# A new written-out sequence of steps, and 255 engine choices, in an mLSTM and gated-FFN kernel

## The chip, the cores and the metric

The kernel runs on one core of one Trainium2 chip. The metric is the time of one execution on the device in microseconds, taken as the median of three runs; one more execution was profiled.

## The reference

Two stages follow each other. The first is an mLSTM cell over 4 batches, 8 heads, 768 steps and head size 40; the second is a gated feed-forward layer over the 3072 tokens that the first one gives.

```python
m_new = np.maximum(f_gate[:, :, t] + m, i_gate[:, :, t])
f_stab = np.exp(f_gate[:, :, t] + m - m_new)
i_stab = np.exp(i_gate[:, :, t] - m_new)
C = f_stab * C + i_stab * einsum('bhd,bhe->bhde', vt, kt)
n = f_stab * n + i_stab * kt
h_tilde = einsum('bhde,bhe->bhd', C, qt)
y[:, :, t] = sigmoid(o_gate) * h_tilde / np.maximum(np.abs(n . qt), 1.0)
...
gate = 1.0 / (1.0 + np.exp(-(x @ w_gate)))     # x: 3072 x 320, w_gate, w_val: 320 x 1536
val = x @ w_val
return gate * val @ w_out                      # w_out: 1536 x 320
```

The weights arrive as 64-bit floats, seen by the kernel as pairs of 32-bit words.

## The kernel before, in words

**Tiling.** The 768 steps are cut into 6 chunks of 128 (c = 0 to 5), so there are 24 units (c, b) of one chunk and one batch; unit u is 4c + b. For a unit the attention takes these steps: q and k are turned (`a`, copied out by `ah`), scores are multiplied (`b`) and masked decays multiplied in (`bm`, VectorE, L1110 or L782), they are applied to v (`c`, tile `av`), the sum is normed (`cv`, `cg`, `cr`; `cr` at L842 writes tile `x`), the last 64 columns of `x` are doubled (`cx`, L850), the result is turned (`d`, tile `xt`) and split in a high part `xh` (`dx`) and a low part `xl` (`dy`, L880). Each chunk also updates a state `cst` (`z`, `zm`, `zd`, `za`) from k weighted by the decay (`bk`, L757). Every product of the feed-forward layer is done with high and low parts: w = wh + wl, x = xh + xl, three products of four.

**The feed-forward tiles.** There are 103 tiles, called 0 to 102. Tile n takes 128 of the 1536 columns for two or four batches of a chunk. Its up-projection `t` is 16 matmuls at L951, 256 or 512 columns wide, eight into bank `pg0` and eight into `pg1`. Then follow `ta` (tanh of pg0, ScalarE, L964), `tg` (the gate times pg1, VectorE, L967), `th` (high part, ScalarE or VectorE), `tl` (low part, VectorE or GpSimd, L978) and the down-projection `p`, three matmuls of 320 columns for each batch at L989. `pg0` and `pg1` exist once. So the next tile's matmuls into pg0 need `ta` of this one, and those into pg1 need its `tg`. Chunk 0 has tiles 0 to 3 (batches 0 and 1), 4 to 7 (batches 2 and 3), and 8 to 15 (all four).

**The weights** are decoded piece by piece: step `a` on ScalarE, three steps `b` on VectorE (L540, L544, L548), the high part `d` and the low part `e` (L589, L593, L595). Pieces are called g, v, r for the first three and 3 to 29 for the rest. One piece holds the columns of two tiles.

**What sets the order.** Nothing is scheduled by a program: the string `ORDER` names every step in turn, and each engine gets its instructions in that order. Each engine runs its own list in order and waits where it needs another's result. The table `eng` in `PARAM` says for a step on which engine it stands: p is GpSimd, v VectorE, a ScalarE. A `/` in `ORDER` swaps which of two PSUM banks the next small tile takes. DMAs are issued by SyncE in the order of the list, those of q for the first unit by ScalarE.

Of the kernel before, what the change touches and what calls it, by code (L numbers as in the profile page):

```python
# [28 lines left out]
        'cm1': 'a', 'cp00': 'a', 'cp02': 'v', 'qb2': 'v', 'ro': 'v', 'xd0': 'v', 'bk0': 'p', 'cx0': 'v', 'bk1': 'p',  # L29
        'cr1': 'v', 'cx1': 'v', 'wve': 'p', 'w3e': 'p', 'w4e': 'p', 'w5e': 'v', 'w6e': 'v', 'w7e': 'p', 'w8e': 'p',  # L30
        'w10e': 'v', 'w11e': 'v', 'w13e': 'v', 'w16e': 'v', 'w17e': 'p', 'w18e': 'p', 'w19e': 'p', 'w20e': 'v',
        'w21e': 'p', 'w23e': 'p', 'w25e': 'p', 'aq2.0': 'v', 'ah2.1': 'a', 'aq2.1': 'v', 'ah2.2': 'a', 'bk2': 'p',
        'cr2': 'p', 'cx2': 'p', 'zm2.1': 'v', 'aq3.0': 'v', 'ah3.1': 'a', 'aq3.1': 'v', 'cr3': 'p', 'zm3.1': 'a',
        'aq4.0': 'v', 'ah4.1': 'v', 'aq4.1': 'v', 'aq4.2': 'p', 'bd4': 'v', 'cr4': 'v', 'dx4': 'v', 'aq5.0': 'v',
        'ah5.1': 'a', 'bk5': 'v', 'zd5.1': 'p', 'tl1': 'p', 'tl2': 'p', 'tl10': 'p', 'arg': 'a', 'w24e': 'p',
        'w27d': 'a', 'za4.0': 'v', 'zm5.0': 'v', 'za5.0': 'v', 'zm5.1': 'a', 'ah6.0': 'a', 'ah6.2': 'v', 'aq6.2': 'v',
        'bd6': 'p', 'za6.0': 'p', 'zd6.1': 'v', 'ah7.0': 'a', 'ah7.1': 'a', 'ah7.2': 'a', 'bk7': 'v', 'cx7': 'p',
        'zm7.0': 'a', 'zd7.0': 'p', 'za7.0': 'p', 'aq8.0': 'a', 'aq8.2': 'v', 'bd8': 'v', 'cr8': 'p', 'cx8': 'v',
        'zm8.0': 'v', 'zd8.0': 'p', 'zm8.1': 'v', 'zd8.1': 'p', 'za8.1': 'v', 'aq9.0': 'a', 'e9a': 'p', 'dx9': 'a',
        'zm9.0': 'a', 'zd9.0': 'p', 'za9.0': 'v', 'zd9.1': 'v', 'aq10.0': 'a', 'cr10': 'p', 'zm10.1': 'v',  # L40
# [1167 lines left out]
```

## Time and profile before

| what | us |
|---|---|
| median of 3 runs (lowest to highest) | 514.95 (514.45 to 516.51) |
| the profiled execution: its time, its span | 513.81, 511.8 |
| TensorE busy with matmuls | 503.7 |
| TensorE loading weights (beside the matmuls) | 458.4 |
| VectorE, ScalarE, GpSimd busy | 318.6, 200.8, 164.3 |

The span goes from the first to the last instruction; the time has 2.0 us around it. Busy time of one engine lies beside that of the others. A matmul's end is modelled, so a busy TensorE is not one at its peak.

### The profile page before, as it was taken

The page shows a single profiled execution, that of the slowest core. Times are in us where ns is not written, and L with a number is a line of the kernel's source. Part 1 is how long each engine was busy: PE and PEld are TensorE (multiplying, and loading weights), DVE is VectorE, ACT ScalarE, POOL GpSimd, SP SyncE. Part 2 cuts the span into 40 slices and gives each one's busy share as a digit, 9 for nine tenths or more (in the row PEclk, how much of TensorE's full clock was granted, in tenths as well). Part 3 has the DMA queues.
Part 4 walks back from the last instruction along what each step waited for, and adds up shares of the span by engine and source line. Part 5 has one row for each costly group of instructions (what it writes and reads, how often), then busy time and mean ns, then how long its engine had stood idle before and what let it go on. Part 6 is the DMA issues. An engine that isn't in the chain of part 4 may idle for free.

```text
span 511.8 us, 12224 instructions
## 1 busy us (share of the span) xinstructions
PE 503.7 (98%) x4671; PEld 458.4 (90%) x4671; DVE 318.6 (62%) x767; ACT 200.8 (39%) x530; POOL 164.3 (32%) x226
## 2 busy tenths in 40 slices
PE   7899999999999999999999999999999999999997
PEld 6788988889999999988888888888888888999997
DVE  8899998997647667565867366676444434442222
ACT  5987765674423332353332322213432411222321
POOL 3563334557730231342225322432241311101111
PEclk9999999999999999999999999999999999999999
DMA  9997768789889695977887788769759730000000
GB/s 196 240 274 192 200 192 221 168 141 189 191 179 172 136 216 119 199 150 156 186 161 180 146 189 195 160 127 190 165 118 198 155 87 5 27 28 1 28 0 27
DMA packets 227578, 75.55 MB, mean 148 GB/s; under 512 B 207040, under 2 KB 215424, under 8 KB 227520
## 3 DMA queue, kind: packets, MB, share of 16 engines
q1 hardware_dynamic: 226432, 74.51, 66.4%
q8 instruction: 37, 0.61, 0.5%
q10 hardware_dynamic: 1088, 0.26, 0.3%
q14 instruction: 21, 0.17, 0.1%
HBM read 57.61 MB, written 17.14 MB: 146 GB/s over the span
## 4 chain that ended last, share of the span: by engine, by line
PE 94%; DVE 3%; DMA 1%; issue 0%; ACT 0%; SPq 0%; DVEq 0%; ACTq 0%
PE pg L951 53%; PE po L989 25%; PE av L754 3%; PE in L797 3%; PE s L776 2%; PE s L771 2%; PE cs L902 2%; PE xt L867 1%; DVE gin L1178 1%; DMA gin<-in_f_gate_dram 1%; DMA st<-in_moe_w_val_dram 1%; PE s L1105 0%; PE pt L639 0%; DVE dc L548 0%; DVE x L842 0%
## 5 line engine op out<-in xcount | busy, mean ns | idle before, releaser
L964 ACT ACTIVATE sg<-pg 128x256 f32<-128x256 f32 (+1 forms) x103 | 48.3, 469 | 221.5 <-PE pg L951 214.8
L967 DVE SCALAR_TENSOR_TENSOR sg<-sg,pg 128x256 f32<-128x256 f32 (+1 forms) x103 | 53.7, 522 | 106.1 <-ACT sg L964 62.7
L951 PE MATMUL pg<-xh,wh 128*128 128x256 f32 (+1 forms) x412 | 112.2, 336 | 0.0
L951 PE MATMUL pg<-xl,wh 128*128 128x256 f32 (+1 forms) x412 | 109.6, 332 | 0.1
L951 PE MATMUL pg<-xh,wl 128*128 128x256 f32 (+1 forms) x412 | 106.2, 329 | 0.0
L978 POOL TENSOR_TENSOR gl<-sg,gh 128x256 fp32r<-128x256 f32 (+1 forms) x51 | 48.9, 958 | 178.2 <-ACT gh L972 61.3
L989 PE MATMUL po<-ol,gh 128*128 128x320 f32 x288 | 87.6, 316 | 0.0
L989 PE MATMUL po<-oh,gh 128*128 128x320 f32 x288 | 87.6, 315 | 0.0
L989 PE MATMUL po<-oh,gl 128*128 128x320 f32 x288 | 86.9, 318 | 0.0
L951 PEld LDWEIGHTS pg<-xl,wh 128*128 128x128 f32 x412 | 70.5, 188 | 6.7 <-DVE xl L880 0.3
L951 PEld LDWEIGHTS pg<-xh,wl 128*128 128x128 f32 x412 | 69.2, 188 | 5.4
L951 PEld LDWEIGHTS pg<-xh,wh 128*128 128x128 f32 x412 | 70.0, 188 | 4.3 <-ACT sg L964 0.5
L951 PE MATMUL pg<-xl,w 128*128 128x256 f32 (+1 forms) x206 | 60.7, 331 | 0.0
L989 PEld LDWEIGHTS po<-oh,gl 128*128 128x128 f32 x288 | 53.2, 188 | 3.2
L989 PEld LDWEIGHTS po<-oh,gh 128*128 128x128 f32 x288 | 53.3, 188 | 3.0
L989 PEld LDWEIGHTS po<-ol,gh 128*128 128x128 f32 x288 | 53.3, 188 | 2.8
L951 PE MATMUL pg<-xh,w 128*128 128x256 f32 (+1 forms) x206 | 54.4, 329 | 0.0
L782 DVE TENSOR_TENSOR d<-s,d 128x384 f32<-128x384 f32 (+1 forms) x66 | 33.1, 506 | 23.1 <-PE s L776 20.3
L972 ACT ACTIVATE gh<-sg 128x256 fp32r<-128x256 f32 (+1 forms) x58 | 28.8, 497 | 42.5 <-DVE sg L967 33.4
L490 ACT ACTIVATE d<-d,at 128x128 f32<-128x128 f32 x136 | 42.8, 390 | 0.0
L951 PEld LDWEIGHTS pg<-xl,w 128*128 128x128 f32 x206 | 36.7, 188 | 2.2
L951 PEld LDWEIGHTS pg<-xh,w 128*128 128x128 f32 x206 | 35.1, 188 | 2.8
(153 smaller groups left out, 712.9 us busy)
## 6 DMA issues: line engine op xcount, KB each, us to landing
d<-mscr SPq DMA_DIRECT2D x22, 512.0 KB
k<-in_k_dram SPq DMA_DIRECT2D x24, 160.0 KB
v<-in_v_dram SPq DMA_DIRECT2D x24, 160.0 KB
o<-in_o_gate_dram SPq DMA_DIRECT2D x24, 160.0 KB
st_o<-in_moe_w_out_dram SPq DMA_DIRECT2D x12, 320.0 KB
scr0q<-qt SPq DMA_DIRECT2D x32, 120.0 KB
scr1q<-qt SPq DMA_DIRECT2D x32, 120.0 KB
out_dram<-ob SPq DMA_DIRECT2D x24, 160.0 KB
```

The source lines that it names most:

```text
L490: nc.scalar.activation(d[:, h, :], d[:, h, :], AF.Exp, bias=at[:, c, b * H + h : b * H + h + 1], scale=-1.0)
L754: nc.tensor.matmul(dst[xs], lhs[:, xs], rhs, start=True, stop=True)
L771: nc.tensor.matmul(ps[g][:, :nh, :], sop[u][:r, g, 0, :], sop[u][:r, g, 1 : 1 + nh, :], start=True, stop=True)
L776: nc.tensor.matmul(ps[g][:, m, :], ks[: 3 * D, h0 + m, :], qs[: 3 * D, h0 + m, :], start=True, stop=True)
L782: nc.vector.tensor_tensor(x, ps[g][:, :nh, :], x, ALU.mult)
L797: nc.tensor.matmul(pi[:, h0 : h0 + nh, :], qk[u][:r, g, :], cst[:r, b, g, : nh * DA], start=True, stop=True)
L951: nc.tensor.matmul(pg[x], w[:, a, fs] if a < 2 else w[:, fs], y[c][:, a, n0:n1], start=first, stop=a == 2 and y is xl)
L964: nc.scalar.activation(sg[0], pg[0], AF.Tanh, scale=0.5)
L967: nc.vector.scalar_tensor_tensor(sg[0], sg[0], 1.0, pg[1], ALU.add, ALU.mult)
L972: nc.scalar.activation(gh[u][:, :nt], sg[0], AF.Copy)
L978: E('gl0' if c == 0 else 'gl', f'tl{n}').tensor_tensor(gl[u][:, :nt], sg[0], gh[u][:, :nt].bitcast(F32), ALU.subtract)
L989: nc.tensor.matmul(po[t], g[c, j, t0][:, (t - t0) * P : (t - t0 + 1) * P], o[:, j, :], start=j == 0 and first, stop=j == NF - 1 and last)
```

## The change

The change touches `eng` and `ORDER` alone. The first 28 steps of `ORDER` stay as they were, all steps behind them stand in another sequence, each as often as before, with nine `/` fewer. Of the engine choices 255 differ. No step is added or left out, and no size, pool or formula differs. Two lines of each table show the manner of it:

```diff
-        'cm1': 'a', 'cp00': 'a', 'cp02': 'v', 'qb2': 'v', 'ro': 'v', 'xd0': 'v', 'bk0': 'p', 'cx0': 'v', 'bk1': 'p',
-        'cr1': 'v', 'cx1': 'v', 'wve': 'p', 'w3e': 'p', 'w4e': 'p', 'w5e': 'v', 'w6e': 'v', 'w7e': 'p', 'w8e': 'p',
+        'cm1': 'a', 'cp00': 'a', 'cp02': 'a', 'qb2': 'v', 'ro': 'v', 'xd0': 'v', 'bk0': 'v', 'cx0': 'p', 'bk1': 'p',
+        'cr1': 'v', 'cx1': 'p', 'wve': 'v', 'w3e': 'p', 'w4e': 'p', 'w5e': 'v', 'w6e': 'p', 'w7e': 'v', 'w8e': 'p',
...
-w26f w25f w29f w28f w21f iw ip*2 it if ii lq0 lk0 ib x0 x1 v1 lk1 lq1 iy ig v0 ig im ia ir is ig im ih igs iac ih
-x2 gc sp00 gc g ex00 lv0 sp01 lo1 tr01 ig ex01 g mk00 tr02 lo0 tr00 cp01 wga mk01 cp02 sc01 cp00 wgb bk0 wva im
+w26f w25f w29f w28f w21f iw ip*2 it if ii lq0 lk0 ib x0 x1 v1 lk1 lq1 iy ig v0 ig im ia ir is ig ie v7 x4 x2 im gc
+iac gc ig ih igs gc tr02 tr00 ih cp02 g tr01 lo1 wga sp10 cp01 im gc wgb lv0 wva sp01 g iq ex01 sp11 wvb lo0 wgb
```

What this does to the engines is seen in their lists at three places.

**VectorE behind the first scan of the gates** (`m` is the running maximum of the first chunk, `mm` its two halves for the matmuls that spread it, `gin`, `mg` and `mend` belong to the gates of the later chunks, `kq` are q and k turned, `dc` is a weight piece in decoding, st its raw words). Before:

```order
L1178 SCALAR_TENSOR_TENSOR m_98<-gin,mend 32x128
L420 CAST mm<-m_98 32x128
L449 COPY at<-pt_ia__156 128x32
L423 TENSOR_TENSOR mm<-m_98,mm 32x128
L1178 SCALAR_TENSOR_TENSOR gin<-mg,gin 32x128
L1178 TENSOR_TENSOR gin<-gin 32x128
L1178 SCALAR_TENSOR_TENSOR gin<-mg,gin 32x512
L1178 TENSOR_TENSOR mend<-gin,m_98 32x1
L1178 TENSOR_TENSOR gin<-gin 32x512
L659 COPY kq_0_220<-pt_0_0_197 120x512
L659 COPY kq_0_220<-pt_0_0_209 80x384
```

The same place in the changed kernel:

```order
L1178 SCALAR_TENSOR_TENSOR m_98<-gin,mend 32x128
L1178 SCALAR_TENSOR_TENSOR gin<-mg,gin 32x128
L449 COPY at<-pt_ia__156 128x32
L1178 TENSOR_TENSOR gin<-gin 32x128
L1178 TENSOR_TENSOR mend<-gin,m_98 32x1
L420 CAST mm<-m_98 32x128
L1178 SCALAR_TENSOR_TENSOR mg<-gin,mend 32x128
L423 TENSOR_TENSOR mm<-m_98,mm 32x128
L1178 SCALAR_TENSOR_TENSOR gin<-mg,gin 32x512
L1178 TENSOR_TENSOR mend<-gin,mg 32x1
L540 TENSOR_SCALAR dc_0_205<-dc_0_205 128x512
L1178 TENSOR_TENSOR gin<-gin 32x512
```

Four instructions of the second chunk's gates now stand ahead of the finished `mm`, and the two copies of `kq` have left this list.

**ScalarE's first instructions** (`d` holds a unit's decays, `mb` the spread maximum, `warm` a tile of zeros that nothing reads later). Before:

```order
L362 DMA qpad_89<-in_q_dram 128x8x40
L1085 ACT_TABLE_LOAD
L1085 ACTIVATE d_0_113<-mb_0_178,at 128x128 x4
L1085 ACTIVATE d_0_113<-mb_1_190,at 128x128 x4
L535 ACTIVATE dc_0_222<-st_0_130 128x512
```

In the changed kernel:

```order
L362 DMA qpad_89<-in_q_dram 128x8x40
L1178 ACT_TABLE_LOAD
L1178 ACTIVATE warm<-warm 1x1
L661 ACTIVATE kq_0_195<-pt_0_0_185 80x384
L535 ACTIVATE dc_0_205<-st_0_130 128x512
L661 ACTIVATE kq_0_195<-pt_0_0_198 120x512
```

The load of the table now belongs to a step on `warm`, which needs nothing from the gates, and the two copies of `kq` stand here.

**VectorE from the gate of tile 1 on** (`sg` is the gate's tile, `w` the third weight piece, `gl` the low part of a tile's result, `d` times `s` are the scores of units 2 and 3). Before, up to the first norm of unit 2:

```order
L967 SCALAR_TENSOR_TENSOR sg_1_0_598<-sg_1_0_598,pg_0_1_0_566 128x256
L782 TENSOR_TENSOR d_2_301<-s_0_2_602,d_2_301 128x256
L589 TENSOR_TENSOR wl_107<-dc_1_526,wh_106 128x2x256
L782 TENSOR_TENSOR d_2_301<-s_0_2_631,d_2_301 128x384
L659 COPY kq_3_518<-pt_0_3_638 80x384
L540 TENSOR_SCALAR dc_2_642<-dc_2_642 128x320
L838 SCALAR_TENSOR_TENSOR av_2_653<-o_2_556,av_2_653 128x8x40
L829 TENSOR_SCALAR den_2_696<-av_2_653 128x8
```

In the changed kernel, from the gate of tile 1 to beyond that norm:

```order
L967 SCALAR_TENSOR_TENSOR sg_1_0_602<-sg_1_0_602,pg_0_1_0_574 128x256
L1178 TENSOR_TENSOR mend<-gin,mg 32x1
L593 TENSOR_TENSOR w_105<-dc_1_479,w_105 64x256
L593 TENSOR_TENSOR w_108<-dc_1_479,w_108 64x256
L1178 SCALAR_TENSOR_TENSOR mg<-gin,mend 32x128
L829 TENSOR_SCALAR den_2_688<-av_2_643 128x8
L832 SCALAR_TENSOR_TENSOR den_2_688<-av_2_643,den_2_688 128x8
L838 SCALAR_TENSOR_TENSOR av_2_643<-o_2_505,av_2_643 128x8x40
L835 RECIPROCAL den_2_688<-den_2_688 128x8
L978 TENSOR_TENSOR gl_1_0_705<-sg_1_0_602,gh_1_0_696 128x256
```

The two low parts at L593 and the one at L978 stood on GpSimd before.

## Rows read from the trace of the kernel before

**Rows 1.** The page: span, busy time of each engine

```profile
span 511.8 us, 12224 instructions
...
PE 503.7 (98%) x4671; PEld 458.4 (90%) x4671; DVE 318.6 (62%) x767; ACT 200.8 (39%) x530; POOL 164.3 (32%) x226
```

**Rows 2.** Busy time of each engine in four stretches (from:to, length, engines, clock, DMA)

```profile
0.00:5.19 5.19, 3.94 (x18) 3.69 (x18) 3.22 (x10) 0.00 (x0) 2.50 (x17) 1.00 0.74 138
5.19:52.96 47.77, 44.24 (x536) 37.79 (x536) 44.48 (x122) 40.20 (x115) 21.56 (x30) 1.00 0.97 237
52.96:122.00 69.04, 69.04 (x574) 59.58 (x573) 62.28 (x150) 45.05 (x121) 32.65 (x39) 1.00 0.78 182
122.00:508.50 386.50, 386.50 (x3548) 357.33 (x3546) 208.64 (x488) 115.08 (x294) 107.57 (x140) 1.00 0.62 131
```

**Rows 3.** What TensorE waited for: us in total, times, longest

```profile
PE xt L867 <- DVE x L842: 1.0, 2, 0.5
PE s L1105 <- DVE kq L659: 0.8, 1, 0.8
```

**Rows 4.** Timeline of the opening: start, length, engine, line, operation, [idle before it]

```profile
3.86 0.41 DVE L1178 TENSOR_TENSOR_SCAN gin<-ones,gin 32x128 f32<-32x128 f32 x1 [0.58 <-DMA gin<-in_f_gate_dram]
...
5.54 0.28 DVE L423 TENSOR_TENSOR mm<-m,mm 32x128 fp32r<-32x128 f32 x1
5.59 1.28 ACT L1085 ACT_TABLE_LOAD   x1 [5.59 <-DVE at L449]
...
9.08 0.91 PE L1105 MATMUL s<-kq 120*128 120x384 f32 x2 [0.78 <-DVE kq L659]
...
9.85 0.84 POOL L757 TENSOR_TENSOR k<-k,d 128x320 f32<-128x320 f32 x1
...
10.12 0.84 DVE L544 TENSOR_SCALAR dc<-dc 128x512 int32<-128x512 int32 x1
...
12.41 0.41 DVE L544 TENSOR_SCALAR dc<-dc 128x512 int32<-128x512 int32 x1
```

**Rows 5.** Timeline of VectorE at the first norm and at the gate step of tile 5

```profile
16.54 0.17 DVE L829 TENSOR_SCALAR den<-av 128x8 f32<-128x8 f32 x1 [1.09 <-PE av L754]
...
52.96 0.41 DVE L967 SCALAR_TENSOR_TENSOR sg<-sg,pg 128x256 f32<-128x256 f32 x1
```

**Rows 6.** Timeline of TensorE: end of tile 0, starts of tile 4 and of tile 6's pg1, last matmul

```profile
27.30 0.36 PE L951 MATMUL pg<-xl,w 128*128 128x256 f32 x1
...
46.16 0.50 PE L951 MATMUL pg<-xh,wh 128*128 128x256 f32 x2
...
53.20 0.40 PE L951 MATMUL pg<-xl,wh 128*128 128x256 f32 x2
53.44 0.48 PE L951 MATMUL pg<-xh,wh 128*128 128x256 f32 x2
...
508.19 0.31 PE L989 MATMUL po<-oh,gl 128*128 128x320 f32 x1
```

**Rows 7.** Forms on VectorE and on GpSimd: count, busy us, mean ns, idle before

```profile
L757 DVE TENSOR_TENSOR k<-k,d 128x320 f32<-128x320 f32 x9 | 4.5, 498 | 0.7 <-POOL d L511 0.6 <-PE pt L644 0.2
L593 DVE TENSOR_TENSOR w<-dc,w 64x256 fp32r<-64x256 f32 x4 | 1.7, 420 | 0.1
L978 DVE TENSOR_TENSOR gl<-sg,gh 128x256 fp32r<-128x256 f32 x30 | 13.0, 432 | 7.2 <-ACT gh L972 4.9 <-PE po L989 1.7
L575 DVE CAST wh<-dc 128x512 fp32r<-128x512 f32 x1 | 0.4, 426 | 0.0
...
L757 POOL TENSOR_TENSOR k<-k,d 128x320 f32<-128x320 f32 x11 | 9.0, 816 | 1.2 <-POOL d L511 0.8
L978 POOL TENSOR_TENSOR gl<-sg,gh 128x256 fp32r<-128x256 f32 x32 | 24.0, 750 | 108.2 <-ACT gh L972 36.1 <-DVE gh L974 30.7 <-PE po L989 26.4
```

**Rows 8.** The same warming matmul at the start and later: count, busy us, mean ns

```profile
L1052 PE MATMUL pwarm0x<-warm 128*128 128x128 f32 x16 | 3.8, 430 | 1.3 <-DVE warm L1178 1.3
...
L1052 PE MATMUL pwarm2x<-warm 128*128 128x128 f32 x4 | 0.6, 274 | 0.0
```

More of the change, by code (lines that the diff above doesn't have):

```diff
@@ L269 @@
[L269 to L271 removed]
+w26f w25f w29f w28f w21f iw ip*2 it if ii lq0 lk0 ib x0 x1 v1 lk1 lq1 iy ig v0 ig im ia ir is ig ie v7 x4 x2 im gc
+iac gc ig ih igs gc tr02 tr00 ih cp02 g tr01 lo1 wga sp10 cp01 im gc wgb lv0 wva sp01 g iq ex01 sp11 wvb lo0 wgb
+tr10 wvb ex11 wgb sp00 wvb / sc01 ex00 gc mk11 cp10 tr11 lv1 mk01 wra cp11 sc10 cp00 mk00 lq2 wrb wvd sc00 bk0 ex10
@@ new lines @@
+zd4.1 t10 w19e k1d t10 lv5 bm5.0 p9*2 ta10 w16f p9 w22e t10 p9 lq7 w20a p8 tg10 p8 p9 t11 k1d t11 za4.1 w24a p8 k1d
+p8 w20b p9 p8 w21b p9 b5.1 w20b th10 t11 w21b t11*2 p9 tl10 w21d t11 w20f t11 lk9 w20b t11 w21e a6.2 t11*2 w20d
+a8.0 t11*2 ah6.2 t11 w24b ah8.0 t11 cx4 p10*2 w24b t11 w20e p10*2 ta11 t11 w24b p10*2 w23a p10 al8.0 p10 e7 p9
+bm5.1 p9 as8.3 p9 / ci5 tg11 w23f t12 zd5.0 e6 cf5 t12*2 w23b as8.2 aq6.0 t12*2 w23b as8.0 t12 th11 lo8 d4 t12
+aq5.2 dx4 p10 w23b t12 w25a t12 zd5.1 t12*2 tl11 w23d v5 p11 b5.2 lo7 w25b za4.0 t12*2 dy4 t12*2 bm5.2 w23e t12
@@ new lines @@
+ah9.1 bk6 p13*3 w29b p12 al9.1 p13 w29b p13*2 d5 t15 aq7.2 as9.6 bm6.2 dx5 t15*2 tg14 as9.7 w28d t15 za5.0 as9.5
+b6.0 ct6 dy5 aq8 w28e w29b t15 aq8 t15 aq8 t15 e7m t15 lq10 bm6.0 b6.1 w29d th14 t15*3 a9.0 t15 tl14 z6 bm6.1 t15
+zm6.0 zm6.1 lk8 t15 w29e t15 as9.4 a7.1 ah9.0 c6 ah7.1 lq12 ta15 al9.0 p13 cs6 ld9 t15 a7.0 as9.1 p14 tg15 ah7.0
+bk7 t16*4 cv6 p13 th15 p14 aq7.1 t16*2 p14 t16 tl15 p14*2 t16 aq7.0 t16 p15 t16*2 cg6 t16*3 cv6 t16 a8.1 t16 p15
+ta16 p15 / b7.1 cv6 oh0 cr6 ah8.1 p14 o0 p15 tg16 e8a p15 cx6 as9.2 p14 al8.1 p14 b7.0 bm7.1 as8.5 p14 as8.6 p14
@@ new lines @@
+t55 al17.1 th54 t55*2 as17.7 zm15.1 t55 tl54 t55 as17.2 p53 ci16 as18.1 p53*2 v18 za15.1 p53*2 za15.0 t55*2 p53
+zd16.1 p54 p53 t55*4 p54 t55*3 p54 t55 p54*2 ta55 p54 t55 z16 oh8 tg55 o8 p53 zm16.0 p54 zm16.1 p54 as17.4 t56
+za16.1 p53 as17.5 p54 t56 lk18 oh10 t56 p54 / b16.0 o10 t56 bm16.0 as17.6 t56 p54 as17.0 t56 th55 t56*2 tl55 t56*2
+zd16.0 t56 oh9 t56*2 p55 o9 t56 p55 lo18 t56 p55 lo16 p55 ta56 p55*3 e17 t56 p55*2 tg56 p54 t57*2 e18a oh11 e17m
+t57*2 th56 o11 t57*2 lk19 ct17 t57 / b16.1 as17.3 e18 tl56 t57 as18.0 bm16.1 t57*2 cf16 t57*3 za16.0 as18.2 t57*2
@@ new lines @@
+e18m / b16.2 lv18 t57 ta57 bm16.2 p55 p56 ct16 a18.1 as18.3 c16 tg57 s17 t58 v22 t58 s17 p55*2 s17 p56 th57 p56 s17
+t58*2 ah18.1 lq19 tl57 t58*2 aq17 t58 cs16 aq17 t58*2 cv16 t58 cv16 aq17 t58 cv16 bk17 t58*2 cg16 t58*2 cr16 t58
+ta58 p57 lv17 a19.1 p56 cx16 p56*2 al18.1 p56*2 tg58 t59*2 p57*2 t59*2 p57 as18.7 p56*3 as18.4 p57 p56 th58 p57
+t59*2 ah19.1 as18.6 t59 tl58 t59*2 as18.5 t59*2 aq18 t59*2 aq18 t59*2 ld19 t59 lq20 ta59 p58 p57 p58 p57 p58*2
+p57*2 b17.2 b17.0 bm17.2 p58*2 a19.0 p58 t60 b17.1 tg59 ah19.0 t60*3 al19.0 t60 al19.1 t60 as19.3 p57 bm17.0 p57
@@ new lines @@
+p63 dy18 p63 ah22.1 t65*2 th64 ct19 al22.1 p63 za18.1 t65*2 p63*2 t65 tl64 p63 t65*3 b19.2 t65 bm19.2 b19.1 a21.0
+t65*2 p63 p64 ta65 b19.0 p64 ah21.0 t65 bm19.0 s20 p64 t66 bm19.1 t66 p64 tg65 / c19 th65 t66 ld21 cs19 t66*2
+al21.0 p64*2 tl65 t66 as21.1 t66*2 lo20 cv19 p65 cv19 p64 as21.3 cv19 p65 cg19 t66*2 zd19.1 cr19 t66*2 p65 cx19
+p64*4 p65 aq20 t66*2 s20 t66 d19 aq20 ta66 z19 dx19 t66 a21.1 zm19.1 p65 v21 p65*2 zm19.0 p65 dy19 t67*2 e22 tg66
+t67*2 p64 za19.0 t67*2 ah21.1 p65 th66 t67 al21.1 t67 tl66 t67*2 as21.6 t67 as21.2 t67 p65 as21.0 t67*2 e21a t67
@@ new lines @@
+cv20 p69 p68 ta70 p68*2 p69 ah22.0 p69 p68 t70 al22.0 p69 t71 tg70 t71 as22.0 t71*2 ld23 th70 t71 o15 t71 cg20 t71
+tl70 cv20 t71 cv20 t71 cr20 t71*2 a23.1 t71 al23.0 t71*4 as23.3 ta71 p69 p70 as22.3 p69*2 ct22 p69 as23.1 tg71
+p69*4 t72 th71 t72*2 as23.0 tl71 p70 t72*2 as22.1 t72*3 cx20 as22.2 t72 e21m t72*2 lv22 t72*5 ta72 b21.0 ci21
+bm21.0 t73 tg72 t73 p70 t73 cf21 t73*2 b21.1 p70*2 bm21.1 p70 p71*3 p70 b21.2 p70*2 s22 p70 t73 aq22 t73 p70 s22
+p70 t73 th72 s22 t73 bm21.2 s22 t73 tl72 t73 lo23 t73*4 d20 ta73 c21 dx20 e22a p71 cs21 p71 t73 t74 cv21 p71 cv21
@@ L272 @@
+p95 th97 t98*4 tl97 t98*11 p96 ta98 p97 p96*2 tg98 t99*3 th98 t99*4 tl98 t99*8 p97*2 ta99 p97 t99 p97*2 tg99 t100*4
+th99 t100*3 tl99 t100*5 p98 t100*4 p98 ta100 p98*3 tg100 p98 t101*2 th100 t101*3 tl100 t101*2 p99 t101*9 p99 ta101
+p99*3 tg101 p99 t102*2 th101 t102*5 tl101 t102*8 p100*2 ta102 t102 p100*2 tg102 p100*2 p101 th102 p101*2 tl102 p101
+p102 p101 p102*2 p101 p102 oh22 p102*2 o22 oh23 o23
 """
```

266 lines of the change are left out of this document (115 added, 151 removed), and 149 rows, old and new, of the table PARAM.

## The prediction

> **What bounds the kernel now.** I read the page first, then the busy time by stretches, TensorE's waits, and the timelines of the opening. The page says that TensorE is busy for 503.7 of 511.8 us [rows 1]. That busy share could hide a bad stretch, so the second view cuts the span where it changes. From 52.96 us to the last matmul TensorE is busy without a gap, 69.04 of 69.04 us and 386.50 of 386.50 us. In the opening it is not: from 5.19 to 52.96 us it lacks 47.77 - 44.24 = 3.5 us, and before that 1.3 us [rows 2]. The third view names its waits, the copies `kq` and the normed tile `x` [rows 3]; the 1.3 us at the start are for the zeros of the warming matmuls [rows 8], which the change does not touch. So matmul time that is the same before and after makes up the whole span, but for some 5 us of gaps, nearly all in the first 45 us. **More than that can't be gained by an order; any amount can be lost by one.**
>
> The reader should see one thing more in the second view. In the opening VectorE is busy 44.48 of 47.77 us, as full as TensorE, and ScalarE 40.20; GpSimd has 21.56. From 122 us on VectorE has 208.64 of 386.50 us and everything but TensorE has room [rows 2]. So the engine choices matter in the opening alone, and there the question is what they do to VectorE.
>
> **Step 1, up to the first result of the attention.** The load of the activation table took 1.28 us and lay between the gates and the first decays, ending at 6.87 us [rows 4]. In the new order it hangs on `warm` and lies before 5 us, at no cost, behind the wait for the gates. Against that, VectorE does four more gate instructions before `mm`: a scan of 128 (0.41 by its sister, [rows 4]), two small ones and another scan, about 1.1 us after overlap. `mm` is finished near 6.9 us instead of 5.82 [rows 4]. Meanwhile TensorE turns q and k, and ScalarE copies `kq` in the time that it had idle. The 0.78 us wait for VectorE's copy [rows 4] goes. Walking VectorE's list on from there without a gap, the scores of unit 0 are done near 15.9 us. Before, TensorE had finished `av` at 16.5 us, when VectorE's 1.09 us wait for it ended [rows 5]; the new one finishes it near 16.8, but VectorE then has a weight piece and a score to do instead of waiting. The two chains come out within 0.4 us of each other.
>
> **Step 2, tile 0 to tile 4.** Tile 0's last matmul began at 27.30 us [rows 6]. In the new list its 16 matmuls stand together behind `xl` of unit 1 (near 23.4 us) with only one turn between, and end near 25.8; but two turns of unit 3, some 0.9 us of matmuls, have moved behind it. Net gain 1.0 us. Following TensorE's, VectorE's and ScalarE's lists on to tile 4, with durations of the forms in the trace, I find TensorE ready to start it between 43.5 and 44.5 us, with the same matmuls done, where it started at 46.16 [rows 6]. That is a gain of 1.7 to 2.6 us, made of the waits for `kq` and `x` [rows 3] and of smaller ones.
>
> **Step 3, what VectorE allows.** Here the engine choices count against the change. I counted VectorE's instructions ahead of the gate step of tile 5, in both orders. Added are two decay weights of k (0.50 each), one third weight piece (2 x 0.42), two low parts `gl` (0.43 each) and a copy `wh` (0.43) [rows 7], two smaller copies of the output weights, and rows that stood later before, such as one spread of q (0.68). That is 9.2 us of additions. Taken away are 5.2 us: other copies of `kq`, two of `x`, a part of the state update. The sum is +4.1 us of durations. Neighbouring instructions overlap: before, 53.3 us of durations made 3.22 + 44.48 = 47.70 us of busy time [rows 2], a factor of 0.9. So VectorE gets **3.7 us more** to do before that gate step.
>
> It began at 52.96 us [rows 5], so VectorE had been idle 52.96 - 47.70 = 5.26 us. Of that 5.19 - 3.22 = 1.97 us lie ahead of 5.19 us [rows 2], mostly the wait for the gates' transfer [rows 4], which stay. The rest, 3.29 us, is what the new order can fill. If it fills all of it, the gate step begins at 47.70 + 3.7 + 1.97 = 53.4 us, 0.4 later than before. Before, the matmuls that wait for it, tile 6's into pg1, began at 53.44, 0.07 us after its end at 53.37 [rows 5, 6], so they can't come earlier than 53.4 + 0.41 + 0.05 = 53.85. TensorE has some 0.9 us more of other matmuls done by then (more down-projections stand between the two tiles). The gain left at this point is 53.44 - 53.85 + 0.9 = **0.5 us**, not the 2 of step 2.
>
> One term is bounded only: the GpSimd work that leaves, some 0.75 to 0.82 us for each of five or more instructions [rows 7]. VectorE's rows of one form last longer with GpSimd beside them: a shift of 128x512 took 0.84 us beside GpSimd's weighting of k, and 0.41 us alone [rows 4]. The relief can't be below 0. Above, it can't exceed the 4 us that leave GpSimd; I take 0.5. Gaps that the new order does not fill go the other way; the walk to tile 4 left about 0.3 us. That gives **+0.7 us of gain** (0.5 + 0.5 - 0.3). Later gate steps allow more: by tile 9 the surplus of work is still 4.2 us of durations, but that step's reader began 2.5 us after its end.
>
> **Step 4, the rest.** From 122 us on the new lists have 12 us less of VectorE's and 10 us more of ScalarE's durations, and some 5 more of GpSimd's. I price this at nothing, since TensorE is gapless there and the others have room [rows 2]. If that cover were gone it would show where `pg0` is taken again. Two 256-column matmuls take 0.24 us from start to start [rows 6]; with such pitches the matmuls between the last into pg0 and the next tile's first take at least 0.85 us in nine of ten tiles in both orders, against `ta` and its latency. Distances from a tile's end to its `p` shrink a little in the chunks 0 and 1 and grow in the others. The transfers keep their distances, 8.6 us or more from the last load of a unit's turned q and k to its scores. The last matmul stays the end; the two stores behind it keep their 3.3 us.
>
> [...] In the new order TensorE has more idle time between 10 and 13.5 us than before, about 2 us in two pieces, waiting for `kq` of unit 1. [...]
>
> **The rivals.**
> - *VectorE decides, and the new order has the gaps of the old.* Then the gate step of tile 5 keeps the 3.3 us of gaps that can be filled, less the 1.09 at `av`, which the list itself shows filled: 53.4 + 2.2 = 55.6 us, and the end moves by 2.2 - 0.5 = 1.7 us, to 516.6; with all 3.3 us, by 2.8, to 517.8. For it: VectorE was full before and gets more. Against: the lists put ready work where the waits were. It decides once the unfilled gaps and the missing relief pass 1.0 us together.
> - *The gain of step 2 is kept.* GpSimd's relief is 2 us instead of 0.5 and TensorE never waits for a gate step: -2.6 us, 512.3, and down to 511 if also the wait at 41 us and later ones go. For it: five transfers of work off GpSimd; against: step 3.
> [...]
> - *The change moves nothing* because everything gained waits at the next gate step: 515.0. Its time is in the forecast's own range.
>
> **How the numbers follow.** The profiled execution took 513.81 us, its span 511.8; that is 1.1 below the median 514.95, as far as one run differs from the next. The sum is a difference, so I apply it to the median: 514.95 - 0.7 = 514.2 us. A measurement of this kernel can tell about 0.5%, 2.6 us, from no change, so same is 512.4 to 517.5. Chances: forecast with "moves nothing" 0.55 (own range 513.2 to 515.5), step 2 kept 0.24, VectorE 0.15, clock 0.06. Of "step 2 kept" some 0.15 lies below 512.4 and of VectorE's 0.09 above 517.5. The 8-in-10 range reaches from 512.0, where most of step 2 is kept, to 517.0.
>
> **What would show it.** Step 1: the table load before 5 us, `mm` near 6.9, no wait of VectorE for `av`. Step 2: tile 4's first matmul at 43.5 to 44.5 us. Step 3: VectorE busy over 50 us ahead of tile 5's gate step, and that step near 53.5 or a little earlier; tile 6's pg1 right behind it. Step 4: no gap of TensorE behind 55 us. The prediction is wrong if TensorE has gaps in the chunks 1 to 5, or if VectorE's instructions are much shorter with less on GpSimd.

## The result, and the profile after

The changed kernel takes 518.25 us (median of 5 runs, 518.04 to 519.17); the kernel before took 514.98 beside it (514.45 to 516.51). The ratio is 1.0063 (95% interval 1.0050 to 1.0075): 3.3 us slower, and the interval lies clear of 1. Forecast were 514.2, with a range of 512.0 to 517.0. The profiled execution took 519.17 us, its span 517.2, the longest of the five; the one of before [rows 1] was shorter than all of its median's runs. So of the 5.4 us between the two profiles some 2 are the difference of two executions.

The page of the changed kernel, as in [rows 1]:

```profile
span 517.2 us, 12219 instructions
...
PE 507.1 (98%) x4671; PEld 460.0 (89%) x4671; DVE 312.7 (60%) x746; ACT 208.5 (40%) x551; POOL 165.9 (32%) x235
```

Busy time in four stretches of the changed kernel (columns as in [rows 2]: from:to, length, then TensorE, its weight loads, VectorE, ScalarE, GpSimd, clock, DMA). The cuts are the gate steps of tile 5 and tile 15:

```profile
0.00:5.19 5.19, 3.93 (x17) 3.66 (x17) 3.20 (x11) 1.49 (x2) 2.57 (x18) 1.00 0.76 132
5.19:54.84 49.65, 46.62 (x545) 40.27 (x544) 46.45 (x130) 39.21 (x113) 16.95 (x24) 1.00 0.93 231
54.84:118.27 63.43, 62.66 (x520) 51.95 (x520) 56.56 (x133) 41.78 (x109) 31.48 (x40) 1.00 0.76 179
118.27:511.00 392.73, 390.99 (x3578) 361.66 (x3577) 204.83 (x471) 125.24 (x325) 114.89 (x154) 1.00 0.61 132
```

The stretch between the same two gate steps in the kernel before:

```profile
52.96:114.51 61.55, 61.55 (x466) 52.64 (x465) 56.75 (x136) 41.05 (x110) 27.09 (x33) 1.00 0.76 183
```

Two things are to be seen. TensorE, gapless behind 52.96 us before [rows 2], now lacks 0.8 us up to tile 15 and 1.7 behind it. And between the two gate steps VectorE is busy for the same time (56.56 against 56.75 us) in a stretch that is 1.9 us longer: it is idle for 6.9 instead of 4.8.

What TensorE waits for now (us in total, times, longest; as [rows 3]):

```profile
PE xt L867 <- DVE x L850: 1.4, 1, 1.4
PE s L771 <- DVE x L842: 1.4, 1, 1.4
...
PE s L1105 <- ACT kq L661: 0.7, 1, 0.7
...
PE pg L951 <- DVE sg L967: 0.3, 1, 0.3
PE po L989 <- DVE gl L978: 0.3, 1, 0.3
PE pg L951 <- ACT sg L964: 0.2, 1, 0.2
```

The first of these lies at 282 us, in chunk 3, far behind the part to which the forecast gave its attention. VectorE's and GpSimd's timelines there (start, length, engine, line, operation):

```profile
281.70 0.49 DVE L842 TENSOR_TENSOR x<-av,den 128x320 f32<-128x320 f32 x1
282.23 2.04 DVE L850 COPY x<-x 128x64 f32<-128x64 f32 x1
284.19 0.79 DVE L693 STREAM_TRANSPOSE kr<-k 128x320 f32<-128x320 f32 x1
```

```profile
282.05 0.32 POOL L896 TENSOR_TENSOR cst<-cst,cdec 80x82 f32<-80x82 f32 x1
282.33 1.89 POOL L495 TENSOR_TENSOR d<-at,d 128x1024 f32<-128x1024 f32 x1
```

and TensorE's:

```profile
282.53 0.38 PE L867 MATMUL xt<-ident,x 128*128 128x128 f32 x2
284.32 0.33 PE L867 MATMUL xt<-ident,x 128*128 128x128 f32 x1 [1.41 <-DVE x L850]
```

A copy of 64 columns, 0.20 us in the middle of this kernel's eight on VectorE, ends at 284.27, just behind GpSimd's multiplication (284.22), and the turn of `x` waits for it. When its record starts GpSimd is still in L896, and L495 follows right behind. Before, this copy (step `cx15`) stood on GpSimd, and the multiplication (step `e17a`) 19 steps later.

The second wait lies at 39.31 us. VectorE's list ahead of it in the changed kernel, with `den`, `av`, `x` of unit 2:

```profile
35.92 1.19 DVE L1178 TENSOR_TENSOR_SCAN mg<-gin,mend 32x128 f32<-32x128 f32 x1
37.04 0.13 DVE L829 TENSOR_SCALAR den<-av 128x8 f32<-128x8 f32 x1
...
37.99 0.78 DVE L978 TENSOR_TENSOR gl<-sg,gh 128x256 fp32r<-128x256 f32 x1
38.69 0.48 DVE L842 TENSOR_TENSOR x<-av,den 128x320 f32<-128x320 f32 x1
```

A scan of the later chunks' gates, which took 0.41 in [rows 4], and a low part of tile 1, 0.43 in [rows 7], stand ahead of the product that TensorE needs, and both are stretched.

Of the small rows, `po` (100.37 us) and `pg` for ScalarE's `ta` (102.42 us) lie in the third stretch; the 0.3 us for VectorE's gate lie at 169 us. What VectorE itself waits for, at the head of its list, from 57 to 118 us in the changed kernel:

```profile
DVE kq L659 <- PE pt L644: 1.6, 2, 0.9
DVE ct L917 <- ACT ct L913: 1.1, 1, 1.1
DVE av L810 <- PE av L754: 1.1, 2, 0.6
DVE wl L589 <- ACT wh L573: 0.8, 1, 0.8
```

In the kernel before the longest single wait there is 0.7 us:

```profile
DVE dc L540 <- ACT dc L535: 1.0, 3, 0.5
DVE t L801 <- PE in L797: 0.7, 1, 0.7
DVE d L782 <- POOL k L757: 0.6, 1, 0.6
```

### The profile page after: what moved, and what is told of

Its sections match the earlier page's. It is cut to its first block, busy times and chain, and to the rows that moved or that the text cites. A ratio compares the mean times of both kernels' runs of the same rounds, so it can differ in the third digit from the quotient of the medians.

```text
span 517.2 us, 12219 instructions
## 1 busy us (share of the span) xinstructions
PE 507.1 (98%) x4671; PEld 460.0 (89%) x4671; DVE 312.7 (60%) x746; ACT 208.5 (40%) x551; POOL 165.9 (32%) x235
## 4 chain that ended last, share of the span: by engine, by line
PE 87%; DVE 6%; issue 2%; DMA 2%; POOL 2%; ACT 1%; ACTq 0%; DVEq 0%; POOLq 0%
PE pg L951 49%; PE po L989 23%; PE av L754 3%; PE s L776 2%; PE in L797 2%; PE cs L902 2%; PE s L771 1%; PE xt L867 1%; DMA qpad<-in_q_dram 1%; DVE dc L548 1%; DMA v<-in_v_dram 1%; PE pt L642 1%; DVE sg L967 1%; DVE dc L544 0%; DVE x L850 0%
## 5 line engine op out<-in xcount | busy, mean ns | idle before, releaser
L951 PE MATMUL pg<-xh,wl 128*128 128x256 f32 (+1 forms) x412 | 109.6, 333 | 0.0
L951 PE MATMUL pg<-xh,wh 128*128 128x256 f32 (+1 forms) x412 | 109.0, 334 | 0.5 <-DVE sg L967 0.3
L978 POOL TENSOR_TENSOR gl<-sg,gh 128x256 fp32r<-128x256 f32 (+1 forms) x55 | 53.0, 964 | 171.9 <-ACT gh L972 76.4
L951 PE MATMUL pg<-xl,wh 128*128 128x256 f32 (+1 forms) x412 | 107.7, 332 | 0.0
L989 PE MATMUL po<-ol,gh 128*128 128x320 f32 x288 | 88.9, 316 | 0.0
L989 PE MATMUL po<-oh,gl 128*128 128x320 f32 x288 | 87.4, 316 | 0.3 <-DVE gl L978 0.3
L989 PE MATMUL po<-oh,gh 128*128 128x320 f32 x288 | 86.3, 314 | 0.0
L989 PEld LDWEIGHTS po<-oh,gl 128*128 128x128 f32 x288 | 53.5, 188 | 3.9 <-DVE gl L978 0.9
L989 PEld LDWEIGHTS po<-oh,gh 128*128 128x128 f32 x288 | 53.3, 188 | 3.8
L989 PEld LDWEIGHTS po<-ol,gh 128*128 128x128 f32 x288 | 53.8, 188 | 3.1
L511 POOL TENSOR_SCALAR_AFFINE_SELECT d<-d 128x1024 f32<-128x1024 f32 x22 | 25.0, 1138 | 41.2 <-ACT d L490 28.7
## 6 DMA issues: line engine op xcount, KB each, us to landing
d<-mscr SPq DMA_DIRECT2D x22, 512.0 KB
```

What stands on the lines that cost most here:

```text
L511: nc.gpsimd.affine_select(out=d, in_=d, pattern=[[0, H], [1, L]], compare_op=ALU.is_ge, fill=0.0, base=0, channel_multiplier=-1)
L951: nc.tensor.matmul(pg[x], w[:, a, fs] if a < 2 else w[:, fs], y[c][:, a, n0:n1], start=first, stop=a == 2 and y is xl)
L978: E('gl0' if c == 0 else 'gl', f'tl{n}').tensor_tensor(gl[u][:, :nt], sg[0], gh[u][:, :nt].bitcast(F32), ALU.subtract)
L989: nc.tensor.matmul(po[t], g[c, j, t0][:, (t - t0) * P : (t - t0 + 1) * P], o[:, j, :], start=j == 0 and first, stop=j == NF - 1 and last)
```

## The experiments

Each kernel was timed beside the kernel before on the same chip, whose medians lay between 514.43 and 515.12 us.

| run | what it is | median us | ratio to before (95%) |
|---|---|---|---|
| e1 | new sequence, old choices | 523.01 | 1.0163 (1.0147 to 1.0179) |
| e2 | old sequence, new choices | 521.72 | 1.0155 (1.0131 to 1.0179) |
| e3 | old up to tile 16, new behind | 518.03 | 1.0069 (1.0057 to 1.0082) |
| e4 | new up to tile 17, old behind | 515.73 | 1.0028 (1.0013 to 1.0043) |
| e5 | changed, one copy on GpSimd | 516.68 | 1.0037 (1.0025 to 1.0049) |
| e6 | changed, `e17a` later in `ORDER` | 517.41 | 1.0060 (1.0040 to 1.0081) |
| e7 | changed, `x` of unit 2 earlier | 517.65 | 1.0059 (1.0034 to 1.0083) |
| e8 | changed, a weight step later | 518.66 | 1.0077 (1.0057 to 1.0097) |
| e9 | changed, four waits moved | 518.69 | 1.0081 (1.0066 to 1.0095) |
| e10 | new up to tile 8, old behind | 521.97 | 1.0147 (1.0128 to 1.0167) |
| e11 | e5, e7, e9 and one more place | 515.12 | 1.0017 (1.0008 to 1.0027) |
| e12 | changed, `e17a` earlier | 517.04 | 1.0052 (1.0034 to 1.0071) |
| e13 | changed, three waits moved | 517.65 | 1.0054 (1.0036 to 1.0071) |
| e14 | e11 with e13's three moves | 514.31 | 0.9995 (0.9980 to 1.0009) |
| e15 | before, table load early | 514.83 | 1.0002 (0.9989 to 1.0016) |

**The two halves of the change.** e1 keeps the new `ORDER` and takes the old `eng`, e2 the reverse; the tables are the two of the diff above, whole.

> The new sequence of steps with the engine choices of before. Theory A, the engine choices are what costs (VectorE gets more to do ahead of tile 5's gate step): most of the 3.3 us between the medians (514.98 and 518.25) goes, so 515.0 to 516.0, with VectorE's busy time ahead of tile 5's gate step back near 47.7 us. Rival B, the sequence costs: 517.5 to 519. If the two only fit together, slower than the changed kernel, over 519.

> The old sequence with the new engine choices. Theory A (choices cost): 517 to 518.5. Rival B (the sequence costs): 514.5 to 515.5. If each set of choices fits only its own sequence: over 518.5, with waits of TensorE spread over the chunks 1 to 5.

Both fell outside theories A and B, in the third case that each text names: each half alone costs 7 to 9 us, more than twice the whole change. Up to 60 us TensorE lacks 6.9 us in e1 and 7.9 in e2, where it lacked 4.8 before; from there to 122 us 1.9 and 0.5, where it lacked nothing. The choices belong to their sequence, and neither half can be called the cause.

**The two stretches of the program.** e3 and e4 cut both `ORDER` and `eng` at a tile, the first step of a tile being the seam:

```diff
-(changed kernel up to t16) t16 ...
+(kernel before up to t16) t16 (what is left, in the changed kernel's order and with its choices)
```

> Sequence and choices of before up to tile 16's first matmul (chunk 0, near 114 us), those of the change behind it. In the profiles the changed kernel has lost 2.8 to 3.5 us by there, and some 2 more behind (0.5 at 168 us, 1.6 at 282 us, where the copy of x on VectorE took 2.04 us). Theory C, the opening chunk decides what the medians show: 515.0 to 516.0. Rival D, the later part decides: 517 or more.

> Sequence and choices of the change up to tile 17's first matmul, those of before behind it: the opposite of the third. Theory C: 517.3 to 518.3. Rival D: 515 to 516. If the 1.6 us at 282 us come in every run, this one lies at 516.5 and the third at 516.5 to 517.

e4 says that the first 17 tiles of the change cost 1.3 us of the 3.3, e3 that the rest costs more: 3.6, of which the seam makes some 0.7 (at 116.15 us TensorE waits 0.93 us for a state piece that ScalarE makes, and 0.2 at this place in the changed kernel). In e3 the copy of unit 15 again took 2.04 us, beside the same multiplication. So theory C, the one nearest to the forecast, falls: on balance more is lost behind chunk 0 than up to its end.

**The copy at 282 us.** e5 undoes one choice:

```diff
-'cx15': 'v'
+'cx15': 'p'
```

> The changed kernel with one of the 255 choices undone: the copy of 64 columns of x for unit 15 (step cx15) on GpSimd again. Theory E, a VectorE instruction is held while GpSimd's long multiplication of the decays (L495, 1.89 us, from 282.33 to 284.22 us) runs, and TensorE's 1.41 us wait for x is that: the wait goes, the copy takes some 0.24 us on GpSimd, and the time falls by 1.4 to 1.6 us, to 516.6 to 516.9. Rival F, the turn of x would have been late or the time is given back later, since something else is behind: under 0.5 us gained.

The wait for `x` at L850 is gone, and 1.57 us with it (518.25 to 516.68). By the ratios to the kernel before it is 1.3 us, and against e6, whose lists are those of the changed kernel (below) and which was timed beside e5, 0.7; the wait in the trace was 1.41. So one of 255 choices is between a fifth and a half of the loss. That the multiplication holds the copy is tried by e6 and e12, which leave the copy where it is. e6:

```diff
-cr15 p53 p52 zd15.1 t54 cx15 e17a p52 a17.1 p52 d15 t54 dx15 p53 t54 ta54 p52 dy15 p52
+cr15 p53 p52 zd15.1 t54 cx15 p52 a17.1 p52 d15 t54 dx15 p53 t54 ta54 p52 dy15 e17a p52
```

and e12, which also takes `e17a` out of its old place:

```diff
-cv15 t54 tl53 cv15
+cv15 t54 e17a tl53 cv15
```

> The changed kernel with the copy left on VectorE, and GpSimd's multiplication L495 (step e17a) issued behind step dy15 instead of right behind the copy. Theory E: the copy takes 0.20 us instead of 2.04, the wait of 1.41 us goes, 516.6 to 516.9 us. Rival G, the copy is slow on VectorE for a reason of its own (its place behind the product x, or a late start): it stays near 2 us and the time at 518.2.

> The changed kernel with the copy of unit 15 left on VectorE, and GpSimd's 1.89 us multiplication L495 put two instructions earlier in its list, where it is over by 281 us. (In the sixth run the move left GpSimd's list as it was, so nothing changed.) Theory E, the copy is held by that instruction: it takes 0.20 us instead of 2.04, and 1.4 to 1.6 us go, 516.6 to 516.9. Rival G, the copy is slow by itself: 2 us and 518.2 again.

e6 tells nothing of the copy: GpSimd has no other step between the two places, so all lists came out the same, and the copy took 2.04 us beside it. It is the changed kernel timed once more: its median is 0.8 us lower, as the medians of the kernel before, five times over, differ by 0.7. In e12 the multiplication ran from 277.44, and the copy:

```profile
281.43 0.19 DVE L850 COPY x<-x 128x64 f32<-128x64 f32 x1
```

0.19 us, and the wait is gone. The medians show 1.2 us of it and the ratios 0.6, within their intervals; the trace decides. Theory E holds: the engine's neighbour, not the engine, made the copy slow.

**The product `x` of unit 2.**

```diff
-ld4 c2 g w7e lk4 g ct2 t2*2
+ld4 c2 g w7e lk4 ct2 t2*2
...
-w8a t2 tl1 b3.1 w4d bk3 cr2 t2
+w8a t2 b3.1 w4d bk3 cr2 g tl1 t2
```

> The changed kernel with two VectorE instructions put behind the product x of unit 2 instead of ahead of it: a scan of the gates (1.19 us at 35.92, of which 0.8 beside GpSimd's mask) and the low part of tile 1 (0.78 us at 37.99). TensorE's 1.38 us wait for x at 39.31 us goes in any case. Theory H, VectorE's sum of work sets tile 5's gate step: that step stays at 54.5 us or later, TensorE waits elsewhere ahead of 60 us, and the time stays within 0.5 us of 518.25. Rival E2, the wait is a loss of its own: tile 4 starts near 45.4 instead of 46.80, tile 5's gate step near 53.5, and the time falls by 1 to 1.4 us.

The 1.38 us went, and a new wait stood 1.5 us ahead of it, for `ta` of tile 2, whose ScalarE waited for the delayed low part:

```profile
37.76 0.50 PE L951 MATMUL pg<-xh,wh 128*128 128x256 f32 x2 [0.89 <-ACT sg L964]
```

Tile 4 starts at 44.68 us and tile 5's gate step at 52.75, some 0.5 to 0.8 us ahead of e5 and e6, whose lists up to there are the changed kernel's. So some 0.5 us is left as gain (0.6 between the medians, within their noise). Theory H's late gate step did not come, and E2's gain of 1 us or more did not either.

**The weight step at 112 us**, 2.05 us long on VectorE (0.49 in the middle of its twelve), beside two instructions of GpSimd that end at 113.81:

```diff
-w28e w29b t15 ... bm6.0 b6.1 w29d th14 t15*3 a9.0 t15 tl14 z6 bm6.1 t15
+w28e t15 ... bm6.0 b6.1 th14 t15*3 a9.0 t15 tl14 z6 bm6.1 w29b w29d t15
...
+'th14': 'a'
```

> The changed kernel with the third step b of weight piece 29 (2.05 us at 112.11 on VectorE, beside GpSimd's low part L595 and mask L511) put behind the scores bm6.1, and the high part of tile 14 on ScalarE. Theory E: the waits of TensorE at 114.2 and 116.3 us (0.25 and 0.41 us) go, and 0.6 to 0.9 us of the time. Rival H, the chunk is bound by the sum of VectorE's work: under 0.3 us gained, with waits in other places.

No gain, and the moved step took 1.23 us in its new place, again beside GpSimd. The two waits went and one of the same size took their place, for a state piece that waits for ScalarE:

```profile
115.84 0.82 PE L754 MATMUL av<-v,d 128*32 128x41 f32 x64 [0.82 <-DVE ct L917]
```

A stretched instruction is no loss in itself: here something else was late as well.

**VectorE's waits at the head of its list.** e9 moves four pieces of the list back by a few places, e13 only the first three. In both:

```diff
-p11 p11 t14*2 w26e lv6 p11 w27e t14*2 tg13 p12
+p11 p11 t14*2 lv6 p11 t14*2 tg13 w26e w27e p12
-zm5.0 zm5.1 t13 w27b p12 ... w27b t13 tl12 t13
+zm5.0 t13 w27b p12 ... w27b t13 tl12 zm5.1 t13
-b6.2 ah7.2 w28b ct7 ... al9.1 p13 w29b p13
+b6.2 w28b ct7 ... al9.1 p13 w29b ah7.2 p13
```

and in e9 alone:

```diff
-a6.0 p8 ah6.0 ct5 ... b5.0 k1c tg9 w19a
+a6.0 p8 ct5 ... b5.0 k1c tg9 ah6.0 w19a
```

> The changed kernel with four places of VectorE's list between 73 and 109 us changed, where it waits at the head of the list while later work is ready: the copies of unit 6's k (idle 0.67 us) behind tile 9's gate step, a state piece (1.13 us) behind the low part of tile 8, a weight piece (0.80 us) behind tile 13's gate step, the copies of unit 7 (0.90 us) behind two weight steps. VectorE does the same work in 57 to 118 us as before the change, with 2.5 us more of idle time. Theory I, these waits are the 2 us lost there: the time falls by 1.3 to 2 us, to 516.3 to 517, and tile 15's gate step comes near 116.5 instead of 118.27. Rival H, the waits only move, as in the eighth run: under 0.5 us gained.

> The changed kernel with three of the four moves of the ninth run: the state piece of unit 5 behind the low part of tile 8, a weight piece behind tile 13's gate step, the copies of unit 7 behind two weight steps. Theory I (single waits at the head of VectorE's list): TensorE's waits at 99.8 and 101.9 us go, and 1.0 to 1.4 us of the time, to 516.9 to 517.3. Rival H (VectorE's sum is the bound and waits only move): within 0.4 us of 518.25.

The "low part of tile 8" in both texts is the step `tl12`, of tile 12.

In e9 the move of `ah6.0` made a wait of its own, since these copies are a score's input:

```profile
PE s L771 <- DVE qc L659: 1.2, 1, 1.2
```

That cancelled what the others gave. In e13 tile 13's gate step is limited by its own `ta` again instead of by a weight piece, and TensorE's waits for `po` at 100 us and for `ta` at 102 us (0.3 and 0.2 above) are gone; the 0.3 us at 169 us stay. Lined up matmul by matmul with the changed kernel (each has the same 4671 records), e13 gains 1.2 us between 60 and 120 us; its median shows 0.6, with an interval of about 0.9 to either side. Theory I is the better one, by the trace more than by the clock on the wall.

**The opening by itself.** e10 was to keep only the new opening:

```diff
-(changed kernel up to t8) t8 ...
+(changed kernel up to t8) t8 (what is left, in the order of before and with its choices)
```

> Sequence and choices of the change up to tile 8's first matmul (near 60 us), those of before behind it. The opening of the change, over the runs so far, stood level with that of before at 60 us, within 0.7 us either way. Theory J, all that is lost lies behind 60 us: 514.3 to 515.3. Rival K, the opening leaves VectorE a backlog that is paid for later, with whatever stands behind: 516 to 517.

It came out at 522 us for a reason of its own, the seam: ScalarE stands still for 9.4 us, from 64.3 to 73.7, waiting for the low part of a weight piece, which it does in neither parent. It says nothing on J or K (of the clock in it more below). e15 took the other way, one part of the opening in the kernel before:

```diff
-is ig im ih igs iac ih
+is ig ie im ih igs iac ih
...
-k0c t4 ie w13a
+k0c t4 w13a
```

> The kernel before with one step moved: the activation on warm (step ie) stands behind the third gate instruction, so the table load of 1.28 us lies ahead of 5 us instead of between the gates and the first decays. If the load is on the path (as step 1 of the prediction took it): the first decays and copies of ScalarE start about 1 us earlier, tile 0 starts up to 0.6 us earlier, 514.1 to 514.5. If q and k, the turns and VectorE's copies bound the opening: no change, 514.4 to 515.0.

No change. The table is loaded from 1.75 us, yet ScalarE's first decays start no earlier, at 6.93 us, where they began at 6.88 right behind the load before: the spread maximum `mb` from TensorE comes only then.

```profile
1.75 1.28 ACT L1178 ACT_TABLE_LOAD   x1 [1.75 <-PEq L1193]
```

**All places together.** e11 and e14 put the edits of e5, e7 and e9 (e14: e13) into the changed kernel, and one more, a state piece ahead of tile 28's gate step at 168 us:

```diff
-zm9.0 t29 zm9.1 t29 ld12 tg28 t29
+zm9.0 t29 t29 ld12 tg28 zm9.1 t29
```

> The changed kernel with the four places of the ninth run, unit 15's copy on GpSimd (1.57 us by the fifth run), the product x of unit 2 earlier (some 0.5 us by the seventh), and a state piece of unit 9 behind tile 28's gate step (TensorE's 0.49 us at 168 us). If the losses are single places that add up: 518.25 - 1.6 - 0.5 - 1.7 - 0.5 = 514 us, 513.5 to 515. If they are not (each place uncovers the next): over 515.5.

> The eleventh run without the move that made its wait of 1.2 us at 74 us. If the places add up: 515.12 - 1.2 = 513.9 us, 513.5 to 514.4, level with the kernel before or up to 1 us below it. If not: 515 or more.

e11 carries the wait of 1.2 us that e9 made, and e14 does not; they differ by 0.8 us. e14, with one choice and seven steps of some 4500 moved, is 3.9 us below the changed kernel, as its text had it, and level with the kernel before (0.9995, 0.9980 to 1.0009). By the medians the named places are the whole loss. Lined up matmul by matmul they are not quite: between 60 and 120 us e14 still lacks some 0.8 us against the kernel before, and some 0.4 behind that. What these are is open.

## Why the prediction was wrong

**Step 4 failed, and with it the forecast.** "I price this at nothing, since TensorE is gapless there and the others have room": busy shares over 386 us [rows 2] say that an engine has time, not that it has it where a matmul waits. Priced at 0, the part behind 60 us cost 4.4 us: that much the changed kernel falls behind the kernel before when their matmuls are lined up, each start against the usual distance of its form (e6: 4.2). 1.6 are the copy at 282 us (e5, e12), 0.5 to 0.7 lie between 120 and 270 us, with the state piece at 168 among them, and 2.1 lie between 60 and 120 us, of which the three moves of e13 give back 1.2. Of that last stretch step 3 said only that "Later gate steps allow more"; yet in [rows 2] VectorE is busy for 62.28 of 69.04 us there, nearly as full as in the opening. Step 4 looked at the bank `pg0`, the distance to `p` and the transfers, and not at the attention's own chain, where TensorE needs `x`, `av` and `kq` without a tile's worth of matmuls between.

**Step 3 had a number that some executions met, from two wrong terms.** It put tile 5's gate step at 53.4 to 53.5 us. Nine profiles have the changed list up to there (the changed kernel's, e4, e5, e6, e8, e9, e10, e12, e13). The step begins between 53.21 (e6) and 55.17 us (e13) in them, at 54.53 in the middle one and at 54.84 in the changed kernel's. VectorE's extra work ahead of it is 1.9 us (3.20 + 46.45 = 49.65 against 47.70), not 3.7. And of the 3.3 us of idle time nothing is filled in four of the nine (the changed kernel's, e4, e9, e13) and 1.0 to 1.4 in the others, not all. The work was over-sized: VectorE's durations ahead of this step sum to 54.4 us before (the prediction had 53.3) and 57.4 now, 3.0 more and not 4.1, and a third of that lies in overlaps, not a tenth. So where the number was met, two errors cancelled; that is luck. The relief from GpSimd, booked as 0.5, was of that size: what VectorE's instructions ahead of this step last beyond the shortest of their line and form sums to 5.9 us before and 5.3 now.

What parts the nine is seen near 20 us, where ScalarE begins a weight piece: at 19.5 to 20.0 us in e5, e6, e8 and e12, and at 20.7 to 21.6 in the others. In e4, e9 and e10 it waits 1.1 to 2.3 us for the piece's transfer, against 0.6 in e5; in the changed kernel's profile and e13 the matmuls had stayed slow for longer: 11 and 10 of them between 7 and 9 us, 21 in e5 (below). The prediction looked at the transfers of q and k alone. This is read from the traces and was not tried.

**Step 2 failed in its place and did not matter.** Tile 4 was to start at 43.5 to 44.5 us; it starts at 46.80, at 45.2 to 45.8 in e5, e6, e8 and e12, and at 46.5 to 47.0 in e4, e9, e10 and e13. The walk had given the scan and the low part of tile 1 their short durations, so it missed the wait of 1.4 us at 39 us; without that wait (e7) tile 4 starts at 44.68.

**Step 1 was right in its parts alone.** The table load lies at 1.76 us, `mm` is finished at 6.77 (forecast 6.9), and VectorE does not wait for `av`. But its sum was not: the score chain came 1 to 2.9 us later than before (first norm at 17.6 to 19.4 us over the runs, forecast 16.8, before 16.54), since ScalarE now copies `kq` first and starts its decays at 11.06, 9.4 in e5; and the load was worth nothing (e15).

Taken together the opening came out about level. Lined up matmul by matmul, the nine profiles stand at 60 us between 0.7 us ahead of the kernel before and 1.2 behind, where a gain of 0.7 was forecast: this term is off by no more than executions differ. It may even have been right. The medians differ by 3.3 us and the part behind 60 us alone costs 4.4, so the median execution should have gained about 1 us in the opening; this is an estimate from the two numbers, and no run shows it.

**The rivals.** The one on the other side named the right engine: VectorE, with unfilled gaps, and its 516.6 to 517.8 was nearest to the result. At tile 5's gate step the gaps did stay in four of nine profiles, but with less work than assumed: 54.8 to 55.2 us instead of 55.6 or later. The loss lies elsewhere: VectorE waiting at the head of its list further on, behind ScalarE and TensorE, and one copy of 2.04 us beside GpSimd's multiplication. A fall of the clock, to which the chances give 0.06, is shown by no run near 12 us: from 11 to 13 us the granted clock reads 1.00 in the changed kernel, e4, e5, e9 and e12.

**The row that should have warned** is in [rows 4]: the shift of 0.84 us beside GpSimd, 0.41 alone. I read it as a tax to be averaged. At 282 us one copy takes 2.04 us beside a multiplication of 1.89, ending 0.05 behind it, and 0.19 without it (e12). At 112 us a weight step of a form with 0.49 in the middle takes 2.05 and ends 0.35 behind GpSimd's mask. What it cost depended on which two met.

## What to carry to other kernels

Where hundreds of choices change at once, a sum of busy time per engine misses the loss, which sits at a few places: walk each chain that TensorE waits for (here `x`, `av`, `kq`), and look at what stands directly ahead of it on its engine, and beside it on GpSimd. An instruction that waits at the head of an in-order list can cost time in a stretch where that engine is nearly full: between 57 and 118 us, three moves at waits of 1.1, 0.8 and 0.9 us gave back 1.2 together. It can cost where the engine has room too, if TensorE's next input stands behind it (0.5 us at 168 us). Moving one back pays only if its own reader is far: the three moves paid together, the fourth made a new wait of 1.2 us. And where executions of one list differ by 2 us in the opening, one profile does not tell whether a forecast of a place was met; several do.

## What the hardware showed beyond that

**The matmuls do not turn from long to short at the same time in every execution.** TensorE's matmuls of 128 columns between 5 and 10 us (count, busy us, mean ns), first in the changed kernel, then in e5, whose list is the same up to there:

```profile
L642 PE MATMUL pt<-ident,qpad 128*120 128x128 f32 x6 | 1.7, 421 | 0.0
```

```profile
L642 PE MATMUL pt<-ident,qpad 128*120 128x128 f32 x6 | 0.9, 273 | 0.0
```

421 ns is what the warming matmuls take at the start in both, and the later ones take 274 [rows 8]: by their durations, the slow stretch lasts to 10.2 us in the changed kernel's profile and to 5.2 us in e5. The granted clock reads 1.00 over both stretches, and in [rows 2]. But the trace's clock records begin only at 10.28 us in the changed kernel, at 5.15 in e5 and at 4.87 in the kernel before, with 1.00; ahead of the first record the view has nothing and counts it as 1.00.

What the longer slow stretch cost in the end is not shown. At 10 us this profile stands some 1.5 us behind e5's. But tile 4 starts at 46.80 us in it and at 46.76 in both e4 and e9, whose records begin at 6.34 and 4.91 us, and tile 5's gate step comes at 54.84, 54.77 and 54.89: by then something else had cost those two as much.

**After holes of 2.75 and 2.37 us the granted clock read 0.50.** In e10 TensorE waited from 61.6 to 64.4 us for a state piece, and from 73.7 to 76.1 for `ta` of a tile; stretches around the two (columns as above, the clock is the seventh figure):

```profile
58.00:61.00 3.00, 3.00 (x25) 2.80 (x24) 2.91 (x10) 1.85 (x6) 0.85 (x4) 1.00 0.19 72
61.00:64.00 3.00, 0.63 (x5) 0.28 (x3) 2.41 (x7) 1.74 (x7) 0.00 (x0) 0.97 0.57 134
64.00:66.00 2.00, 1.62 (x3) 1.01 (x4) 0.00 (x0) 0.33 (x2) 0.00 (x0) 0.50 1.12 203
66.00:70.00 4.00, 4.00 (x12) 3.26 (x11) 1.15 (x2) 0.00 (x0) 0.00 (x0) 0.50 0.79 210
70.00:74.00 4.00, 3.73 (x77) 2.70 (x75) 0.00 (x0) 0.27 (x1) 1.23 (x3) 0.92 0.16 30
78.00:80.00 2.00, 2.00 (x7) 1.54 (x6) 1.87 (x5) 1.27 (x3) 0.00 (x0) 0.50 0.22 22
```

Before the first hole TensorE was busy all the time at 1.00, behind it at 0.50, with twelve matmuls in 4 us; a down-projection matmul (L989) took 0.47 us at 67.96, and 0.31 at 59.70. Between 70 and 74 us the mean was 0.92, and behind the second hole it was 0.50 again. The mean clock was below 0.998 in all five executions of e10. None of the waits of 1.4 us in the changed kernel did this (the clock reads 1.00 from 38 to 41 us and from 282 to 286), nor the 1.7 us at 22.6 us in e4 and e9, whose profiled executions have a mean clock of 1.0.
